# Late q turned by whole rows, and a reordered start, in a linear attention followed by a SwiGLU layer

## The chip, the core and the metric

The kernel runs on one core of a Trainium2 chip. The metric is the device time of one execution in microseconds (us), as the median of several runs; lower is better. Before the change it is 319.28 us, the median of three runs (319.25 to 319.5).

## The reference

Inputs are float32: q, k, v of 8 batches x 8 heads x 576 tokens x 64, a gain for the attention's norm, and the weights of the second layer. First a linear attention without softmax, with a root-mean-square norm over each head's 64 outputs:

```python
kv = np.einsum('bhsd,bhse->bhde', k, v)
out = np.einsum('bhsd,bhde->bhse', q, kv)
rms = np.sqrt(np.mean(out * out, axis=-1, keepdims=True) + 1e-06)
return (out / rms * g_norm).astype(np.float32)
```

Its result, laid out as 4608 tokens x 512, goes through a second norm and a gated feed-forward layer of width 1536:

```python
rms = np.sqrt(np.mean(x * x, axis=-1, keepdims=True) + 1e-06)
xn = x / rms * rms_g
g = xn @ w_gate
silu = g * (1.0 / (1.0 + np.exp(-g)))
val = xn @ w_val
return (silu * val @ w_out).astype(np.float32)
```

## The kernel before, in words

All products are in bf16 with float32 sums. The tokens go through the feed-forward part in nine groups of 512: the first 512 tokens of each of the 8 batches, and a last group of the 8 remainders of 64. Per group there are twelve pairs of a gate product and a value product (four products of 128 rows each, over the 512 channels), a Silu on ScalarE (ACT, L746), a multiplication on VectorE (DVE, L755), and then the output products (L773). While a group's feed-forward products run on TensorE (PE), the attention of the next batch is worked off in between; a planner (`Placer`) deals its operations out to slots. The change does not touch the planner.

For batch 0 there is nothing to hide behind. Its attention is written out by hand, line by line (L866 to L960), and this is the order in which each engine gets its instructions. Every engine works its own list in order; an instruction that waits holds up all that stand behind it on that engine. Batch 0 is done in two halves of 256 tokens: `part` 0 ("early", chunks 0 and 1) and `part` 1 ("late", chunks 2 and 3). The names below are those of the listing.

- `idle_on` (L900) and `spin` (L256) are products whose results nobody reads. `idle_on` takes data that has just landed, so such a product waits for it.
- `kv_pairs` makes k-transposed times v for a pair of heads; `qT_quads` (L325) turns q by products with the identity, in blocks of 64 rows x 64 columns, and `qT_out` (L360) copies the turned q out of PSUM.
- `oT_mm` (L452) makes the attention's output turned, only for the statistics: `sqT_` (L465) squares it on ACT, and `stat_pairs` (L472) sums the squares per head with a small product (L484).
- `o_pairs` (L422) makes the output itself in tiles `ox` and `oy`. `lead_chain` (L518) turns the sums into one factor per token and head: reciprocal, product, sum, product on DVE, a Sqrt on ACT (L533), a reciprocal on DVE. `xna_pairs` (L432) multiplies the output by that factor on DVE; `xT_mm` (L601) turns it on PE and `xT_out` (L614) copies it out, times the gain. Only then can the first gate products start (`gates`, L760).
- The late half goes through the same steps, but its factor is worked out by `chain` (L538), twelve small DVE steps without a Sqrt. `behind` (L985) puts these steps between the early half's feed-forward slots by a table, `steps`: after slot n, steps a to b.

Three PSUM pools bound what may run ahead: `att` (3 tiles), `mm1` (3) and `o2` (2). ACT holds one table of functions at a time: Sqrt's and Silu's differ, and `preload_act_table` (L948) loads Silu's. The weights come in eight transfers, gate and value in turn (`wg`, `wv`, three blocks of 128 columns each), issued by GpSimd (POOL) and converted on the way; all transfers of the start share the DMA engines. PE uses the first block's gate, then its value, then the second's, and so on; the first nine pairs run on the early half alone.

Of the kernel before, what the change touches and what calls it, by code (L numbers as in the profile page):

```python
# [11 lines left out]
BF16 = mybir.dt.bfloat16  # L12
# [75 lines left out]
def kernel(  # L88
# [12 lines left out]
    nc = tc.nc  # L101
    B, H, S, D = q.shape
# [3 lines left out]
    NC = 4  # L106
    MAIN = 128 * NC
# [25 lines left out]
    o2_p = pool("o2", 2, space=bass.MemoryType.PSUM)  # L133
    att_p = pool("att", 3, space=bass.MemoryType.PSUM)


    idle = consts.tile([128, MAIN], BF16, name="idle")
    nc.vector.memset(idle, 0.0)
    ident = consts.tile([128, 128], BF16, name="ident")
# [20 lines left out]
    krT = consts.tile([128, 2, H, D], BF16, name="remk")  # L160
    vr = consts.tile([128, H, 2, D], BF16, name="remv")
# [16 lines left out]
    mains, xs = {}, {}  # L178
# [77 lines left out]
    def spin(ps, n):  # L256
        for _ in range(n):
            nc.tensor.matmul(ps, lhsT=idle[:, :128], rhs=idle[:, : ps.shape[-1]], start=True, stop=True, skip_group_check=True)
# [4 lines left out]
    class Att:  # L263
# [61 lines left out]
        def qT_quads(self, part, halves, pools):  # L325
            tiles = [
                pool.tile([128, 2, MAIN // 2], BF16, name="o2" if pool is o2_p else "att") for pool in pools
            ]
            for c in range(NC):
                for h in range(H // 2):  # L330
                    for ps, hh in zip(tiles, halves):
                        rows, at = slice(hh * D, (hh + 1) * D), slice(h % 2 * D, (h % 2 + 1) * D)
                        nc.tensor.matmul(
                            ps[at, h // 2, c * D : (c + 1) * D],
                            lhsT=mains[0, 0][rows, part, h, c * D : (c + 1) * D], rhs=ident[rows, rows],
                            is_transpose=True, start=True, stop=True, skip_group_check=True,
                        )
            return tiles

        def turned(self):  # L340
            self.qT_ps = [att_p.tile([128, NS, MAIN // 2], BF16, name="att") for _ in range(2)]
            for c in range(NC):
                for h in range(H):
                    for r, ps in enumerate(self.qT_ps):
                        rows, at = slice(r * D, (r + 1) * D), slice(h % 2 * D, (h % 2 + 1) * D)
                        nc.tensor.matmul(
                            ps[at, h // 2, c * D : (c + 1) * D],
                            lhsT=qc[rows, h, c * D : (c + 1) * D], rhs=ident[rows, rows],
                            is_transpose=True, start=True, stop=True, skip_group_check=True,
                        )  # L350
# [517 lines left out]
    V, G, A = nc.vector, nc.gpsimd, nc.scalar  # L868
    H0, H1 = (0, 4), (4, 8)
    P0, P1 = (0, 1), (2, 3)  # L870
# [26 lines left out]
    idle_ps = mm1_p.tile([128, MAIN], FP32, name="mm1")  # L897
    spin(idle_ps, 17)

    def idle_on(rhs, n):  # L900
        for _ in range(n):
            nc.tensor.matmul(
                idle_ps[:, : 4 * D], lhsT=idle[: rhs.shape[0], :128], rhs=rhs,
                start=True, stop=True, skip_group_check=True,
            )

    idle_on(vr[:, 0:2].rearrange("p h c d -> p (h c d)"), 3)
    a = Att(0)
    cast_main(0, 1, V, H0)
    cast_main(0, 1, A, H1)  # L910
    V.tensor_copy(out=krT[: REM // 2], in_=krst.rearrange("p h (c d) -> p c h d", c=2))
    idle_on(mains[0, 1][:, 0, 4:8, :].rearrange("p h d -> p (h d)"), 4)
    idle_on(krT[:, 0, 0:4].rearrange("p h d -> p (h d)"), 2)
    kva = a.kv_pairs(P0)
    for i, j in enumerate(P0):
        a.kv_pairs_out(kva, i, j)
    idle_on(mains[0, 0][:D, 0, 0], 3)
    qa, qb = a.qT_quads(0, (0, 1), (att_p, att_p))
    a.qT_out(qa, P0, 0, A)
    a.qT_out(qb, P1, 0, V)  # L920
# [16 lines left out]
    )  # L937
    a.sqT_(a.oT_mm((3,), 0, 2, o2_p, 2), (3,), 0, 2)
    a.stat_pairs(P0, 0, 2, mm1_p, "mm1", guard=True)
    (la,) = a.qT_quads(1, (0,), (att_p,))  # L940
    a.stat_pairs(P1, 0, 2, mm1_p, "mm1")
    a.qT_out(la, P0, 2, A)
    ox = a.o_pairs(P0, 0, 2, att_p, "att")
    oy = a.o_pairs(P1, 0, 2, att_p, "att")
    a.lead_chain(0, 2, table=False)
    (lb,) = a.qT_quads(1, (1,), (att_p,))
    a.qT_out(lb, P1, 2, A)
    A.preload_act_table(ACT.Silu)  # L948
    xt = [a.xT_ps(1, (0, 1), pool_) for pool_ in (o2_p, None, None)]
    lo = [a.oT_mm(P0, 2, 4, o2_p), a.oT_mm(P1, 2, 4)]  # L950
    spin(mm1_p.tile([128, MAIN], FP32, name="mm1"), 2)
    xt.append(a.xT_ps(1, (0, 1), mm1_p))
    for o, js in ((ox, P0), (oy, P1)):
# [1 line left out]
            a.xna_pairs(o[:, :, 2 * i : 2 * i + 2], (j,), 0, 2)  # L955
    for j in ALL:
        a.xT_mm((j,), (0, 1), ps=xt[j])
        a.xT_out(j, (0, 1), A if j == 2 else V)
    for ps, js in zip(lo, (P0, P1)):
        a.sqT_(ps, js, 2, 4)  # L960

    for t in (0, 2, 1):
        load_cast(1, t, (0, H))
# [14 lines left out]
    for n, w in enumerate(FB):  # L978
        js = range(FB0[n], FB0[n] + w)
        early += [slots_a(0, j, 0, half)[0] for j in js if n] + [slots_a(0, j, 0, half)[1] for j in js]  # L980
    held = {}

    steps = {1: (0, 3), 2: (3, 6), 3: (6, 12)}

    def behind(n):  # L985
        if n == 1:
            a.st = None
            a.stat_pairs(P0, 2, 4, att_p, "att")
            a.stat_pairs(P1, 2, 4, att_p, "att")
        if n in steps:  # L990
            for f in a.chain(2, NC)[slice(*steps[n])]:
                f()
        if n in (3, 4):
            held[n - 3] = a.o_pairs((P0, P1)[n - 3], 2, 4, att_p, "att")
        if n == 6:
            for i, js in enumerate((P0, P1)):
                a.xna_pairs(held[i], js, 2, 4)
        if n in (10, 11):
            js = (P0, P1)[n - 10]
            a.xT_mm(js, (2, 3))  # L1000
            for j in js:
                a.xT_out(j, (2, 3), A)

    def lead(n0, n1):
        for n in range(n0, n1):
            if n == 12:
                gate = nc.sync.dma_start(out=gbc, in_=g_norm.partition_broadcast(128))
                tc.add_manual_dep(gate.ins, w_loads[-1][0].ins.name, SYNC, reason="the weights come first")
            emit([early[n]])
            behind(n)  # L1010
# [74 lines left out]
```

## Time and profile before

| | us |
|---|---|
| median of three runs | 319.28 (319.25 to 319.5) |
| the profiled execution | 319.22 |
| its span, first to last instruction | 317.5 |
| PE busy | 310.1 (98%) |
| DVE, ACT, POOL busy | 167.9, 139.1, 87.5 |

In stretches of the start, busy time of each engine in us (PEld is the loading of weights into PE's array; the DMA column is what the DMA engines moved):

| us of the span | PE | DVE | ACT | POOL | GB/s |
|---|---|---|---|---|---|
| 5 to 10 | 4.05 of 5 | 1.50 | 1.04 | 4.79 | 195 |
| 10 to 15 | 4.53 of 5 | 2.44 | 2.63 | 4.19 | 202 |
| 15 to 20 | 4.27 of 5 | 3.29 | 4.04 | 2.26 | 201 |
| 20 to 25 | 5.00 of 5 | 4.47 | 2.50 | 2.85 | 205 |
| 25 to 30 | 4.81 of 5 | 2.52 | 2.41 | 3.85 | 197 |

How to read the profile: a row of a timeline gives the start and the length in us, the engine, the line of the listing, the operation, the tiles as out<-in, sizes, a count, and in brackets the idle time before it with what ended it. Products on PE overlap, and their ends are modelled, so starts are the safer reading: the distance from start to start is what one costs in a row. The chain of waits goes back from the last instruction, at each step to what released it.

### The profile page before, as it was taken

How to read it: one execution, taken by the hardware profiler on the slowest of the kernel's cores; microseconds unless marked ns; L12 is line 12 of the kernel's file. 1: busy time of each engine (PE TensorE's matmuls, PEld its weight loads, DVE VectorE, ACT ScalarE, POOL GpSimd, SP SyncE). 2: the span in 40 equal slices, each digit the busy share in tenths (PEclk: the TensorE clock that was granted, in tenths of full speed). 3: DMA queues.
4: the chain of work that ended last, by engine and by line, in shares of the span. 5: the costliest groups of instructions: out<-in, count | busy, mean ns of one | idle time of the engine just before them, and what ended most of it. 6: DMA issues, size and time to landing. Idle time of an engine off the chain costs nothing.

```text
span 317.5 us, 5789 instructions
## 1 busy us (share of the span) xinstructions
PE 310.1 (98%) x2252; PEld 157.4 (50%) x2252; DVE 167.9 (53%) x379; ACT 139.1 (44%) x263; POOL 87.5 (28%) x108
## 2 busy tenths in 40 slices
PE   7899999999999999999999999999999999999995
PEld 3688855544454444444544454444444444444443
DVE  5475546579759643854196618561769034103310
ACT  2455364596477324631483237322842233233321
POOL 8846430067018301820085008400510000000000
PEclk9999999999999999999999999999999999999999
DMA  8999999999971994595439955954001600040002
GB/s 201 197 202 199 198 236 197 175 223 142 194 224 13 162 179 154 113 196 131 127 98 142 155 148 139 161 135 133 1 2 22 192 2 2 21 106 8 0 33 99
DMA packets 78358, 40.18 MB, mean 127 GB/s; under 512 B 43000, under 2 KB 73852, under 8 KB 78332
## 3 DMA queue, kind: packets, MB, share of 16 engines
q0 software_dynamic: 32304, 14.75, 36.6%
q1 hardware_dynamic: 45328, 24.48, 32.3%
q10 hardware_dynamic: 700, 0.59, 0.6%
q8 instruction: 17, 0.28, 0.4%
q14 instruction: 9, 0.07, 0.1%
HBM read 37.78 MB, written 9.44 MB: 149 GB/s over the span
## 4 chain that ended last, share of the span: by engine, by line
PE 93%; DMA 2%; ACT 1%; DVE 1%; POOL 1%; issue 1%; DVEq 0%; POOLq 0%
PE mm L737 58%; PE o L773 27%; DMA main_q<-in_q_dram 2%; PE mm L773 2%; PE att L294 2%; PE o L409 1%; PE att L409 1%; DVE xna L436 0%; PE mm L804 0%; PE o L804 0%; PE o L737 0%; PE att L608 0%; ACT x L618 0%; PE mm L766 0%; PE att L384 0%
## 5 line engine op out<-in xcount | busy, mean ns | idle before, releaser
L755 DVE TENSOR_TENSOR h<-silu,mm 128x512 bf16<-128x512 bf16 (+1 forms) x117 | 74.4, 636 | 87.5 <-PE mm L737 78.6
L746 ACT ACTIVATE silu<-mm 128x512 bf16<-128x512 f32 (+1 forms) x119 | 66.3, 558 | 85.6 <-PE mm L737 77.1
L737 PE MATMUL mm<-x,wv 128*128 128x512 bf16 (+1 forms) x420 | 98.2, 358 | 0.2 <-ACT silu L746 0.2
L737 PE MATMUL mm<-x,wg 128*128 128x512 bf16 (+1 forms) x420 | 98.4, 358 | 0.0
L773 PE MATMUL o<-wo,h 128*128 128x512 bf16 x396 | 90.1, 379 | 0.3 <-issue 0.3
L737 PEld LDWEIGHTS <-wv 128*128 128x128 bf16 x480 | 46.4, 98 | 45.7 <-issue 0.4
L737 PEld LDWEIGHTS <-wg 128*128 128x128 bf16 x468 | 45.5, 98 | 46.0
L501 POOL TENSOR_TENSOR sq<-sq,g 128x512 bf16<-128x512 bf16 x28 | 32.0, 1153 | 127.6 <-ACT sq L392 82.0
L773 PEld LDWEIGHTS <-h 128*128 128x128 bf16 x420 | 40.4, 98 | 47.5 <-issue 0.6
L793 ACT COPY osb<-o 128x512 f32<-128x512 f32 x33 | 19.2, 586 | 69.1 <-PE o L773 69.1
L509 DVE TENSOR_REDUCE st<-sq 128x8 f32<-128x512 bf16 x56 | 35.9, 677 | 0.0
L323 DVE CAST kvs<-att 64x256 bf16<-64x256 f32 x14 | 5.9, 422 | 30.8 <-PE att L294 30.6
L578 DVE TENSOR_TENSOR xna<-outa,al 128x512 bf16<-128x512 bf16 x24 | 15.1, 682 | 0.0
L737 PE MATMUL mm<-xr,wg 128*128 128x512 bf16 x48 | 12.3, 379 | 0.0
L737 PE MATMUL mm<-xr,wv 128*128 128x512 bf16 x48 | 12.3, 379 | 0.0
L229 POOL CAST main_q<-stg 128x1024 bf16<-128x1024 f32 x10 | 10.3, 1073 | 0.0
L200 POOL DMA_DIRECT2D vc<-in_v_dram x10 | 8.6, 862 | 2.7 <-DMA wv<-in_moe_w_val_dram 1.6
L893 ACT ACTIVATE wv<-wv,gain 128x384 bf16<-128x384 bf16 x16 | 9.0, 608 | 0.4 <-PE mm L737 0.4
L773 PE MATMUL mm<-wo,h 128*128 128x512 bf16 x24 | 7.6, 379 | 0.0
L446 ACT ACTIVATE sq<-att 128x512 bf16<-128x512 f32 x12 | 7.6, 633 | 0.0
L446 ACT ACTIVATE sq<-o 128x512 bf16<-128x512 f32 x12 | 7.3, 611 | 0.0
L200 POOL DMA_DIRECT2D kc<-in_k_dram x7 | 6.5, 932 | 2.9 <-DMA kc<-in_k_dram 1.7
(146 smaller groups left out, 188.4 us busy)
## 6 DMA issues: line engine op xcount, KB each, us to landing
out_dram<-osb SPq DMA_DIRECT2D x27, 256.0 KB, 2.5
stg<-in_q_dram SPq DMA_DIRECT2D x6, 1024.0 KB, 6.7
vc<-in_v_dram POOLq DMA_DIRECT2D x7, 512.0 KB, 8.1
kc<-in_k_dram POOLq DMA_DIRECT2D x7, 512.0 KB, 6.4
out_dram<-osb SPq DMA_DIRECT2D x17, 128.0 KB, 2.4
wg<-in_moe_w_gate_dram POOLq DMA_DIRECT2D x4, 384.0 KB, 10.4
wv<-in_moe_w_val_dram POOLq DMA_DIRECT2D x4, 384.0 KB, 11.6
wo<-in_moe_w_out_dram POOLq DMA_DIRECT2D x4, 384.0 KB, 14.4
```

Of the source, the lines that this page charges most:

```text
L200: return nc.gpsimd.dma_start(out=to[:, heads[0] : heads[1], : NC * D], in_=view)
L229: return copy(out=mains[b, t][:, cs[0] : cs[1], h0:h1, :], in_=staged[b, t].rearrange("p h (c d) -> p c h d", c=NC)[:, cs[0] : cs[1], h0:h ...
L446: nc.scalar.activation(out=self.sq[c][:, 0], in_=self.o_of(c), func=ACT.Square)
L501: eng.tensor_tensor(out=self.sq[c][:, 1], in0=self.sq[c][:, 0], in1=g2, op=OP.mult)
L509: nc.vector.reduce_sum(out=self.part(self.st[:, which], c), in_=of, axis=AX.X)
L578: return eng.tensor_tensor(out=self.part(self.xna, c), in0=of, in1=self.part(self.al, c).to_broadcast([128, 2, H // 2, D]), op=OP.mult,)
L737: nc.tensor.matmul(ps[:, : c1 - c0], lhsT=w[n][:, s, jj * 128 : (jj + 1) * 128], rhs=x_of(g, s, c0, c1), start=s == 0, stop=s == NS - 1)
L746: nc.scalar.activation(out=sis[g, j][:, c0:c1], in_=ps, func=ACT.Silu)
L755: nc.vector.tensor_tensor(out=hs[g, j][:, c0:c1], in0=sis[g, j][:, c0:c1], in1=v_ps, op=OP.mult)
L773: nc.tensor.matmul(ps, lhsT=hs[g, j][:, t * 128 : (t + 1) * 128], rhs=wo[j // OB][:, j % OB, :], start=j == 0, stop=j == NF - 1)
L793: (eng.copy if eng is nc.scalar else eng.tensor_copy)(out=o, in_=ps)
L893: A.mul(out=w[:, s], in_=w[:, s], mul=gain[:, s : s + 1])
```

## The change

- The first half's idle products: twelve of 256 columns become six of 512.
- Late q is turned by a new function, `qT_halves`: 16 products over all 128 rows in place of 32 in blocks of 64 x 64, into one tile `late` of pool `att`. It stands between `ox` and `oy`; before, one half stood between the two halves of the statistics and the other behind `lead_chain`.
- Both halves of late q are copied out by ACT behind the Sqrt of `lead_chain`; before, the first copy stood ahead of it.
- Late squares (`sqT_` of `lo`) stand ahead of the load of the Silu table; before, behind ACT's copy of the third x. The third of the four x tiles is allocated after `lo`.
- All four first x are copied out by DVE; before, the third by ACT.
- The statistics and the first chain steps of the late half come after slot 0 in place of slot 1, and the steps are dealt out as 4, 2, 2, 4 in place of 3, 3, 6.

```diff
+        def qT_halves(self, part):
+            ps = att_p.tile([128, 2, 2, MAIN // 2], BF16, name="att")
+            for c in range(NC):
+                for h in range(H // 2):
+                    at = slice(h % 2 * D, (h % 2 + 1) * D)
+                    nc.tensor.matmul(
+                        ps[at, :, h // 2, c * D : (c + 1) * D],
+                        lhsT=mains[0, 0][:, part, h, c * D : (c + 1) * D], rhs=ident,
+                        is_transpose=True, start=True, stop=True, skip_group_check=True,
+                    )
+            return ps
...
-                idle_ps[:, : 4 * D], lhsT=idle[: rhs.shape[0], :128], rhs=rhs,
-                start=True, stop=True, skip_group_check=True,
-            )
-
-    idle_on(vr[:, 0:2].rearrange("p h c d -> p (h c d)"), 3)
+                idle_ps, lhsT=idle[: rhs.shape[0], :128], rhs=rhs, start=True, stop=True, skip_group_check=True
+            )
+
+    idle_on(vr[:, 0:4].rearrange("p h c d -> p (h c d)"), 2)
...
-    idle_on(mains[0, 1][:, 0, 4:8, :].rearrange("p h d -> p (h d)"), 4)
-    idle_on(krT[:, 0, 0:4].rearrange("p h d -> p (h d)"), 2)
+    idle_on(mains[0, 1][:, 0].rearrange("p h d -> p (h d)"), 2)
+    idle_on(krT[:, 0].rearrange("p h d -> p (h d)"), 1)
...
-    idle_on(mains[0, 0][:D, 0, 0], 3)
+    idle_on(mains[0, 0][:D, 0, 0:2].rearrange("p h x -> p (h x)"), 1)
...
     a.stat_pairs(P0, 0, 2, mm1_p, "mm1", guard=True)
-    (la,) = a.qT_quads(1, (0,), (att_p,))
     a.stat_pairs(P1, 0, 2, mm1_p, "mm1")
-    a.qT_out(la, P0, 2, A)
     ox = a.o_pairs(P0, 0, 2, att_p, "att")
+    late = a.qT_halves(1)
     oy = a.o_pairs(P1, 0, 2, att_p, "att")
     a.lead_chain(0, 2, table=False)
-    (lb,) = a.qT_quads(1, (1,), (att_p,))
-    a.qT_out(lb, P1, 2, A)
+    a.qT_out(late[:, 0], P0, 2, A)
+    a.qT_out(late[:, 1], P1, 2, A)
+    xt = [a.xT_ps(1, (0, 1), pool_) for pool_ in (o2_p, None)]
+    lo = [a.oT_mm(P0, 2, 4, o2_p), a.oT_mm(P1, 2, 4)]
+    xt.append(a.xT_ps(1, (0, 1)))
+    for ps, js in zip(lo, (P0, P1)):
+        a.sqT_(ps, js, 2, 4)
     A.preload_act_table(ACT.Silu)
-    xt = [a.xT_ps(1, (0, 1), pool_) for pool_ in (o2_p, None, None)]
-    lo = [a.oT_mm(P0, 2, 4, o2_p), a.oT_mm(P1, 2, 4)]
     spin(mm1_p.tile([128, MAIN], FP32, name="mm1"), 2)
...
-        a.xT_out(j, (0, 1), A if j == 2 else V)
-    for ps, js in zip(lo, (P0, P1)):
-        a.sqT_(ps, js, 2, 4)
+        a.xT_out(j, (0, 1), V)
...
-    steps = {1: (0, 3), 2: (3, 6), 3: (6, 12)}
+    steps = {0: (0, 4), 1: (4, 6), 2: (6, 8), 3: (8, 12)}
 
     def behind(n):
-        if n == 1:
+        if n == 0:
             a.st = None
```

## The prediction

> **What bounds the kernel now.** I read the page first (busy shares, chain by line), then the chain of waits from 12.2 to 26.2 us, the timelines of PE, ACT and DVE over the same stretch, and last the issues of the weights with their time to landing.
>
> From the page:
>
> ```profile
> PE 310.1 (98%) x2252; PEld 157.4 (50%) x2252; DVE 167.9 (53%) x379; ACT 139.1 (44%) x263; POOL 87.5 (28%) x108
> ...
> PE 93%; DMA 2%; ACT 1%; DVE 1%; POOL 1%; issue 1%; DVEq 0%; POOLq 0%
> ```
>
> The span is TensorE's products. A change that leaves the products of the feed-forward part alone gains only where PE stands still. From 26.1 us on, the chain is PE products almost without a break, so everything is decided in the first 26 us. The chain of waits there (start, length, what):
>
> ```profile
> 13.11 0.18 PE mm L484 x4
> 13.29 0.37 PE att L333 x16
> 13.66 0.20 PE mm L484 x4
> 13.86 0.02 issue
> 13.88 0.27 DVE r L527
> ...
> 15.40 1.43 DVE xna L436 x4
> ...
> 25.26 0.50 ACT x L618
> 25.76 0.28 ACT silu L746
> 26.05 0.04 issue
> 26.09 0.27 PE mm L737
> ```
>
> The turn of half of late q (L333) lies on the path between the two halves of the statistics (L484); then DVE's chain and the four xna products follow. The end of this stretch is another engine: ACT's four late turns of x (L618) hold back a Silu, and PE waits for that Silu at 26.09. In between stands a transfer. The issues on POOL's timeline (start, length), from the view of DMA issues in a window inside each one its time to landing (last column), and PE's row of the product that uses the second:
>
> ```profile
> 11.08 0.75 POOL L248 DMA_DIRECT2D wg<-in_moe_w_gate_dram  x1
> 11.81 0.76 POOL L249 DMA_DIRECT2D wv<-in_moe_w_val_dram  x1
> ...
> wg<-in_moe_w_gate_dram POOLq DMA_DIRECT2D x1, 384.0 KB, 11.6
> ...
> wv<-in_moe_w_val_dram POOLq DMA_DIRECT2D x1, 384.0 KB, 12.9
> ...
> 24.86 1.03 PE L737 MATMUL mm<-x,wv 128*128 128x256 bf16 x8
> ```
>
> The third gate block lands at 11.08 + 11.6 = 22.68, the third value block at 11.81 + 12.9 = 24.7. PE's first product with the gate block starts at 23.01, with its weight load at 22.91: 0.2 us to spare. Its first product with the value block starts at 24.86 (weight load 24.72), where the products before it (four from 24.33, 0.109 each) would have let it start at 24.77. PE already stands at that landing. Whatever is gained ahead of it can pass only through the wait behind it.
>
> **The change, part by part.**
>
> **Idle products.** Out go 3 + 4 + 2 + 3 = 12 of 256 columns at 0.109 us (1.31), in come 6 of 512 at 0.216 (1.30). The last ones before each real product end ahead of a DMA: v at 8.57 (0.30 of wait in PE's row) and q's second half at 10.06 (the chain's 3.44 + 6.62). Cost 0; without that cover 0.1 at most.
>
> **Statistics in one run.** The 16 turns go from between the halves: 0.37 in the chain. The second half then needs the square of j = 3, which ends at 13.20; the first half ends at 13.29 in the chain. So the second half ends about 0.38 earlier and DVE's reciprocal starts at 13.50 in place of 13.88; if the semaphore of that square comes later than I take it, the gain is 0.34. DVE's chain and Sqrt keep their lengths: Sqrt 14.41 to 14.63 (was 14.79), xna from 15.01 and its last end at 16.43 (was 16.82).
>
> **Late q in whole rows.** 32 products of 64 rows x 64 columns become 16 that take all 128 rows and give 128 columns each. No such row is in the trace. The nearest: L333 itself, 16 in 0.25 without the changes of shape (starts 13.22 to 13.47); L294 (128 rows, 64 columns, two column halves in turn), 40 in 0.76, two per 0.038; L426 (128 columns, no halves) 0.055 each. The bounds for 16 are 0.25 and 16 x 0.055 = 0.88; I take pairs side by side like L294's with L426's width, 8 x 0.057 = 0.46, and two changes of shape of 0.07 to 0.1 (L333's first and last neighbours). It is in PE's order after `ox` and before `oy`: 13.62 to 14.07, read by ACT from about 14.3. `oy` ends by 14.5 (15.0 at the other bound), xna needs it at 15.7: covered.
>
> **Sqrt ahead of both copies.** On ACT before: copy 13.70, Sqrt 14.79, copy 14.92 to 15.48. After: Sqrt to 14.63, copies from 14.53 and 15.01 (start to start 0.12 and 0.48, as L533 to L364 and L470 to L470 show), the second to 15.58. So the second late copy ends 0.10 later although everything else is earlier. What is queued behind it on PE: `lo[1]` (2 x 0.109), the two spins (2 x 0.216), and only then the turns of x. The first turn starts at 16.28 (was 16.18), DVE's first x is then at 16.59 instead of 16.73, released by PE and no longer by its own xna, and ends at 16.93; the gates start at 16.98 instead of 17.13. Of 0.38, **0.15 is left**. If the wide turns run one after another, copies shift 0.14 and nothing is left; if the copies do not overlap (0.57 + 0.57 from 14.63) the second ends at 15.77, 0.04 worse than no gain.
>
> **x of j = 2 on DVE.** ACT loses 0.47, DVE gains 0.26 (its start to start). The fourth x ends at 17.71; the gates need it in their last quarter, nine products after 16.98, at 17.96. Cost 0, with 0.25 to spare.
>
> **Late squares ahead of the Silu table.** ACT: squares from 15.57 and 16.06 to 16.65, the table load (1.28) to 17.94; the first Silu is wanted when the first gate ends, 16.98 + 9 x 0.109 + 0.27 = 18.23. Cost 0, with 0.3 to spare; before, the Silu at 18.50 came straight behind these squares.
> [...]
>
> ```profile
> 15.50 1.28 ACT L948 ACT_TABLE_LOAD   x1
> 17.18 0.47 ACT L618 ACTIVATE x<-att,gain 128x256 bf16<-128x256 bf16 x1 [0.40 <-PE att L608]
> ```
>
> The load starts 0.02 behind the copy before it, and the next ACT operation comes 0.40 behind its end, waiting for PE. So a pause after a load is between 0 and 0.40; I take 0. [...]
>
> **Statistics and chain of the late half one slot earlier.** The 8 products (0.20) stand ahead of the first value block instead of behind it: same PE work. On DVE the four steps (0.2, 0.3, 0.2, 0.2) now run from 18.67, ahead of the first h, which goes from 19.14 to about 19.57; the second h ends at 20.61 (was 20.47). The fifth gate (20.83, waits for DVE) would start at 20.68: it just fits. The late xna starts at 22.07 instead of 22.53, off the path.
>
> **Through the two landings.** The gates' lead of 0.15 survives the gate block (weight load 22.77 against 22.68). At the value block PE still starts at 24.86. But ACT's run that ends at 26.04 begins when that gate's product ends (23.65), so it ends 0.15 earlier; eight products from 24.86 end their issue at 25.74, so PE's next starts at 25.94 instead of 26.09. After that PE runs on without a wait to 41.50, the next transfers being 1 us and more ahead of it. **Sum: 0.15 less.** The profiled execution took 319.22 (span 317.5), the three runs 319.28 in the median, 0.06 more: 319.1 either way.
>
> **The rivals.**
> **A, slower: ACT's queue holds PE.** Either the second late copy ends after 15.73 (then the gates start later than 17.13) or the Silu table is ready after 18.28. [...] Both pass on to the end, since PE has only 0.09 in hand at the value block: 319.3 to 319.5. For it: ACT now has two copies and two squares in a row with PE products queued behind each. Against: the rows show copies overlapping and no pause over 0.40.
> **B, the pause at 41.50 goes or moves.** The chain shows 0.34 of "issue" there (start to start 0.51 more than a product), with no waiting semaphore named; PE has 22 products fewer ahead of it, so it can fall elsewhere. Gone with the 0.15: 319.22 - 0.65 = 318.6. For: nothing in the rows ties it to data. Against: nothing says that it depends on the count.
> **C, the landings come earlier too** or ACT's run shrinks: the whole 0.36 (24.86 + 0.88 = 25.74 to 26.09) plus 0.09 at the value block: 318.8. Against: POOL issues the weights by 13.3, before anything changes.
> **D, much slower: PE's pace.** The windows' table has 7 idle products in 1 to 4 us and 11 in 4 to 6, at a granted clock of 1.00 in both: a half pace that the clock column does not show. If thinner work ahead of 17 us brought it back, it decides from some gap longer than the 0.46 of idle time before 6.79, which left the pace whole; the longest that the change makes is about 0.7 (14.4 to 15.15, `oy` to `lo[0]`). Price: about 2.8 us at half pace (1.2 to 4.0 was needed to leave it), 1.4 lost: 320.6. [...]
>
> **How the numbers follow.** Forecast 0.48 (its own range 319.0 to 319.25), A 0.20, B 0.14, C 0.08, D and further pauses 0.10. About 0.2% (0.64 us) is what a measurement of this kernel can tell from no change. Only B (most of it, 0.11) and a bit of C (0.01) go past it as faster, D as slower: 0.12, 0.78, 0.10. The range takes in the forecast, A with its bounds, C and B's 318.6, up to 319.7 for a pause on top of A; it leaves out D and the far end of B.
>
> **What would show it.** Reciprocal at 13.5; Sqrt at 14.4 with two copies behind; first turn of x not before 16.2; gates at 17.0; the product with the third value block still at 24.8 to 24.9; the Silu wait at 26.09 shortened by about as much as the gates moved. Wrong if that block lands elsewhere, if the wide turns take over 0.9 us, or if a new PE wait above 0.2 stands between 17 and 24 us.

## The result and the profile after

The changed kernel takes 318.62 us in the median of 20 runs (318.3 to 319.15), the kernel before 319.39 in 20 runs beside them: a ratio of 0.9976, 95% interval 0.9969 to 0.9983, or 0.77 us less (0.54 to 0.99). The time lies in the range, at its low end, and on the faster side of the bound of 0.2%, across which the interval reaches. That is the place of rival B, which had a chance of 0.14; the likeliest case had its own range of 319.0 to 319.25 and was missed. The range held because its lower end was set by B. Both profiled executions of experiment 6 ran with PE at a reduced pace (spans 329.1 and 654.5 us), and such executions are left out of the ratios.

The profiled execution took 318.71 us (before 319.22), its span 316.9 (317.5). From its page:

```profile
PE 308.4 (97%) x2208; PEld 156.6 (49%) x2230; DVE 168.1 (53%) x380; ACT 138.8 (44%) x262; POOL 87.6 (28%) x108
...
PE 94%; DMA 2%; ACT 1%; issue 1%; DVE 0%; POOL 0%; POOLq 0%
```

The chain of waits in the start of the changed kernel (start, length, what), with what answers to the rows shown of before:

```profile
13.17 0.40 PE mm L496 x8
13.57 0.02 issue
13.59 0.27 DVE r L539
...
14.50 0.22 ACT nt L545
14.72 0.97 ACT qTs L376 x2
15.69 0.04 issue
15.73 0.38 PE att L471 x2
...
25.73 0.28 ACT silu L758
26.02 0.04 issue
26.06 0.38 PE mm L749 x2
```

The statistics (now L496) are one run of eight, and the reciprocal starts 0.29 earlier. Behind the Sqrt (L545) the chain no longer goes on through DVE's xna: it goes through ACT's two copies of late q (L376) to PE's second pair of late outputs (L471), as the prediction had it. And at 26.06 stands the same wait for a Silu, 0.03 us earlier than before. So the start gave nearly nothing. The half microsecond is elsewhere. The same view around the first output products, first of before, then of the changed kernel:

```profile
41.29 0.21 PE o L773
41.50 0.34 issue
41.85 0.38 PE o L773
42.23 0.22 PE mm L773
```

```profile
41.25 0.21 PE o L785
41.47 0.05 issue
41.52 0.38 PE mm L785
41.90 0.43 PE att L471 x2
```

The pause in which no semaphore is waited for is gone. (The changed trace lacks the record of the second output product; the third starts at 41.52, on time.) To split the difference of the two profiled executions, I take four marks that every kernel has: ACT's first copy of q (10.60 before, 10.66 after), PE's first product behind the Silu wait (26.09, 26.06), the first output product (41.12, 41.09) and the end of the span.

| stretch, us | before | after | difference |
|---|---|---|---|
| up to the first copy of q | 10.60 | 10.66 | +0.06 |
| to the product behind the Silu wait | 15.49 | 15.40 | -0.09 |
| to the first output product | 15.03 | 15.03 | 0 |
| to the end | 276.3 | 275.8 | -0.5 |

The first row is mostly the landing of the first transfers; in the experiments below it lies between 10.3 and 11.5, and it is left out when kernels are compared. Between the first copy and the reciprocal a late landing of v added 0.24 us in experiment 7, and the reciprocal came 0.10 later in experiment 2, so the distance from DVE's reciprocal to the first gate product is the safer reading of the front: 3.24 before, 3.50 in the changed kernel. The two profiled executions differ by 0.51, the medians by 0.77; the interval begins at 0.54, and what lies between is not attributed.

### The profile page after: what moved, and what is told of

It is laid out like the page before. It is cut to its first block, busy times and chain, and to the rows that moved or that the text cites. A ratio compares the mean times of both kernels' runs of the same rounds, so it can differ in the third digit from the quotient of the medians.

```text
span 316.9 us, 5724 instructions
## 1 busy us (share of the span) xinstructions
PE 308.4 (97%) x2208; PEld 156.6 (49%) x2230; DVE 168.1 (53%) x380; ACT 138.8 (44%) x262; POOL 87.6 (28%) x108
## 4 chain that ended last, share of the span: by engine, by line
PE 94%; DMA 2%; ACT 1%; issue 1%; DVE 0%; POOL 0%; POOLq 0%
PE mm L749 58%; PE o L785 27%; DMA vc<-in_v_dram 2%; PE mm L785 2%; PE att L294 2%; PE o L421 1%; PE att L421 1%; ACT qTs L376 0%; PE o L749 0%; PE mm L816 0%; PE o L816 0%; PE att L620 0%; PE att L471 0%; ACT x L630 0%; PE mm L778 0%
## 5 line engine op out<-in xcount | busy, mean ns | idle before, releaser
L785 PE MATMUL o<-wo,h 128*128 128x512 bf16 x382 | 87.5, 379 | 1.1 <-issue 0.6
L749 PE MATMUL mm<-xr,wv 128*128 128x512 bf16 x47 | 12.3, 379 | 0.1
L749 PE MATMUL mm<-xr,wg 128*128 128x512 bf16 x47 | 12.3, 379 | 0.1
```

The lines of the kernel that those rows point to most:

```text
L749: nc.tensor.matmul(ps[:, : c1 - c0], lhsT=w[n][:, s, jj * 128 : (jj + 1) * 128], rhs=x_of(g, s, c0, c1), start=s == 0, stop=s == NS - 1)
L785: nc.tensor.matmul(ps, lhsT=hs[g, j][:, t * 128 : (t + 1) * 128], rhs=wo[j // OB][:, j % OB, :], start=j == 0, stop=j == NF - 1)
```

## Experiments

The question was what the pause hangs on, and what each part of the change does to the front. Ratios are to the kernel before, run beside each; they are not simply the quotients of the medians. Each kernel has one profiled execution from which the stretches are read.

**1. Wide idle products alone.** The kernel before with `idle_on` of the changed one:

```diff
-    idle_on(vr[:, 0:2].rearrange("p h c d -> p (h c d)"), 3)
+    idle_on(vr[:, 0:4].rearrange("p h c d -> p (h c d)"), 2)
...
```

> The kernel before with one part of the change alone: six idle products of 512 columns in place of twelve of 256; all else as before, 6 products fewer on PE. Theory F (the gain is what PE is ahead at the wait for the Silu near 26.1 us): no change, within 0.1 us of before, the Silu wait ends at 26.1 and the pause near 41.4 stays. Theory P (the gain is the pause of 0.5 us between the first two output products near 41.4, and it depends on how many instructions PE has been given before): the pause may move or go with 12 instructions fewer; if it goes, 0.5 us faster. Theory L (that pause comes and goes with the time at which transfers land): it comes and goes without regard to the kernel, and the time is that of before within 0.1 us.

Ratio 0.9988 (0.9976 to 1.0001). The front is that of before to 0.01 (6.53 us from the first copy of q to the gates, 15.49 to the product behind the Silu wait). But the pause has moved. The chain of this kernel:

```profile
42.57 0.22 PE mm L773
42.78 0.22 PE o L773
43.00 0.14 issue
43.14 0.39 PE o L773
```

It is shorter (0.14 of issue) and stands six products further on in the program. Six products fewer had been given to PE.

**2. The changed kernel with the narrow idle products**, the reverse edit.

> The changed kernel with the twelve narrow idle products of before (6 products more on PE than in the changed kernel). F and L: as the changed kernel, 0.7 to 0.8 us faster than before. P: if the pause near 41.4 depends on the count of instructions, it may be back with 12 more, and then only 0.2 to 0.3 us faster than before.

Ratio 0.9979 (0.9966 to 0.9992), no pause, 275.8 from the first output product to the end. Sixteen products fewer than before are enough. The front of this execution was no faster than before (6.53 and 15.53): its reciprocal came 0.10 later after the first copy of q than in the changed kernel, and from there to the gates it took the same 3.50.

**3. The changed kernel with PE's count restored.**

```diff
     spin(idle_ps, 17)
+    spin(idle_ps[:, :16], 22)
```

> The changed kernel with 22 idle products of 16 columns more, behind the first 17 idle products, where PE waits for data anyway: PE's count of products is that of before, 44 instructions more than in the changed kernel. F and L: as the changed kernel, 0.7 to 0.8 us faster than before. P: the pause of 0.5 us near 41.4 is back at the same product, and the kernel is within 0.3 us of before.

Ratio 1.0007 (0.9994 to 1.0019): the whole gain is gone, and the pause is back at the same product, longer than before:

```profile
41.44 0.22 PE o L785
41.66 0.70 issue
42.36 0.39 PE o L785
```

The front is that of the changed kernel to 0.06 (6.49 and 15.45). Counted through each trace, the paused product has the same number in all three kernels that have a pause, though it is another product of the program in the second (number, start, line, tiles; in the changed kernel the same number falls on a product of the statistics):

```
before:         478  41.85  L773 o<-wo,h
wide idle:      478  43.14  L773 o<-wo,h
count restored: 478  42.36  L785 o<-wo,h
changed:        478  44.86  L506 att<-sel,sqT
```

So in these three kernels the pause goes with a place in PE's list of instructions, not with any data. And it is the whole difference behind the first output product: 276.33 less 0.51 before, 276.12 less 0.30 in experiment 1 and 276.69 less 0.87 here (from start to start, beyond a product's own 0.22) are all 275.82, the stretch of the kernels without a pause.

**4. The first parts of the change alone:** wide idle products, late q by whole rows, statistics in one run, Sqrt first; squares, x and chain steps as before.

```diff
-    for ps, js in zip(lo, (P0, P1)):
-        a.sqT_(ps, js, 2, 4)
     A.preload_act_table(ACT.Silu)
...
-        a.xT_out(j, (0, 1), V)
+        a.xT_out(j, (0, 1), A if j == 2 else V)
+    for ps, js in zip(lo, (P0, P1)):
+        a.sqT_(ps, js, 2, 4)
...
-    steps = {0: (0, 4), 1: (4, 6), 2: (6, 8), 3: (8, 12)}
+    steps = {1: (0, 3), 2: (3, 6), 3: (6, 12)}
```

> The changed kernel without its last two parts: late squares stand behind the Silu table again, the third x is copied by ACT again, and the late statistics and chain steps come after slot 1 in 3, 3 and 6 as before. What is left of the change: wide idle products, late q by whole rows, statistics in one run, Sqrt ahead of both copies. F: the gates start as early as in the changed kernel (17.0 to 17.1), but the squares are ACT's again just ahead of the first Silu, so part of the gain at 26.1 goes: 0.3 to 0.8 us faster than before. P and L: PE has the changed kernel's count, no pause near 41.4, at least 0.5 us faster than before.

Ratio 0.9980 (0.9969 to 0.9991), no pause, 6.43 and 15.39 from the first copy of q: the front of the changed kernel to 0.01. The late squares ahead of the table, the third x on DVE and the earlier chain steps are worth nothing here. This kernel also answers what stands behind a table load. ACT's timeline:

```profile
15.88 1.28 ACT L958 ACT_TABLE_LOAD   x1
17.18 0.47 ACT L630 ACTIVATE x<-att,gain 128x256 bf16<-128x256 bf16 x1
```

The load ends at 17.16 and the next operation starts at 17.18, 0.02 later.

**5. The kernel before with 106 products more** and nothing of the change:

```diff
-    spin(idle_ps, 17)
+    spin(idle_ps, 8)
+    spin(idle_ps[:, :64], 115)
```

> The kernel before, with 106 idle products more and nothing of the change: 8 of 512 and 115 of 64 columns in place of the first 17 of 512, about as long in all. [...] Theory W (the 22 products fewer of the change make PE earlier or its list shorter as such): the list is longer, so the pause stays or grows and the time is that of before or more.

No pause; PE's timeline of this kernel runs through the first output products without a gap, two of them in 0.43 us:

```profile
41.57 0.60 PE L737 MATMUL mm<-x,wv 128*128 128x256 bf16 x4
42.01 0.59 PE L773 MATMUL o<-wo,h 128*128 128x512 bf16 x2
42.44 0.38 PE L773 MATMUL mm<-wo,h 128*128 128x512 bf16 x1
```

275.8 to the end, with the old front (6.53 and 15.49). The time is that of before: ratio 0.9996 (0.9983 to 1.0008), since the many small products kept PE busy until 8.81 (6.3 before) and pushed the first copy of q to 11.49, 0.89 later, which gave back what the pause had cost. A longer list without the pause contradicts theory W. The 478th product is another one here and starts at 39.80.

**6. The kernel before with 30 products more**, 16 of 512 and 31 of 16 columns in place of 17 of 512, run twice.

> The kernel before with 30 idle products more (16 of 512 and 31 of 16 columns in place of the first 17 of 512). [...] W: the pause stays where it is, within 0.2 us of before.

> The same kernel as in the run with 30 idle products more, whose profiled execution was at a lower granted clock and cannot be read. [...] W: the pause stands at the same output product as before.

Ratios 1.0000 (0.9988 to 1.0012) and 1.0003 (0.9987 to 1.0020). A pause longer by 1 us than that of before would have shown (0.3%); there is none. Theory W had this time, but where a pause stands, if there is one, can't be seen: no stretch of this kernel can be read. With 30 products more the products ahead of the 478th are others too (see below). Why the time is that of before, and not half a microsecond less, stays open.

**7. Late q by whole rows alone**, at its old place between the halves of the statistics, the first copy ahead of the Sqrt (not shown: the second copy reads the same tile, and the second and third x tiles are allocated after `lo`):

```diff
-    (la,) = a.qT_quads(1, (0,), (att_p,))
+    late = a.qT_halves(1)
     a.stat_pairs(P1, 0, 2, mm1_p, "mm1")
-    a.qT_out(la, P0, 2, A)
+    a.qT_out(late[:, 0], P0, 2, A)
...
```

> The kernel before with late q turned by whole rows alone, at the old place between the halves of the statistics, and the first copy ahead of the Sqrt as before; twelve narrow idle products, squares, table, x and chain as before. 16 products fewer on PE. [...] F (the front makes the gain): 0.1 to 0.2 us slower than before.

Ratio 0.9981 (0.9969 to 0.9992). No pause (275.8), and a front that is slower by 0.47: 7.00 to the gates, 15.96 to the product behind the Silu wait. But 0.24 of that is not the edit's. It stands ahead of the turn, at products that take v, for whose transfer PE waited there in this execution and not in that of before:

```profile
11.26 0.38 PE L310 MATMUL mm<-vc,main_k 128*128 128x128 bf16 x4 [0.44 <-DMA vc<-in_v_dram]
```

The edit's own part is the turn between the halves of the statistics, 0.57 in place of 0.37 in the chain of waits, 0.2 more; from the reciprocal to the gates it is 3.24 as before. A kernel whose start is worse than before is faster than before.

**8. Both copies ahead of the Sqrt**, in the changed kernel:

```diff
-    a.lead_chain(0, 2, table=False)
     a.qT_out(late[:, 0], P0, 2, A)
     a.qT_out(late[:, 1], P1, 2, A)
+    a.lead_chain(0, 2, table=False)
```

> The changed kernel with both copies of late q ahead of the Sqrt on ACT: the step that puts the Sqrt first undone, and nothing else. Late q is turned by 14.3, so the copies hold ACT from about 14.35 to 15.4 and the Sqrt starts 0.8 later than now; the late outputs come 0.3 earlier, but the first x then waits for DVE's xna again: gates at 6.9 to 7.1 from the first copy of q in place of 6.43, the Silu wait behind them later by the same, 0.4 to 0.6 us slower than the changed kernel and 0.1 to 0.4 faster than before, with no pause at the output products (same count). If the order on ACT is worth nothing, as the changed kernel.

Ratio 0.9994 (0.9981 to 1.0006), 7.05 and 16.02: 0.62 behind the changed kernel in both, and 4.12 from the reciprocal to the gates in place of 3.50, with no pause. The Sqrt waits for the copies:

```profile
14.79 1.07 ACT L376 COPY qTs<-att 128x512 bf16<-128x512 bf16 x2 [1.14 <-PE att L345]
15.75 0.23 ACT L545 ACTIVATE nt<-z 128x16 f32<-128x16 f32 x1
```

So this order is what keeps the wide turn from making the front slower.

**9. Without the two idle products ahead of the turns of x**, in the changed kernel (the tile is still taken).

```diff
-    spin(mm1_p.tile([128, MAIN], FP32, name="mm1"), 2)
+    mm1_p.tile([128, MAIN], FP32, name="mm1")
```

> The changed kernel without the two idle products between the late outputs and the first turns of x (0.43 of PE ahead of those turns; 2 products fewer). If PE's order behind the second late copy holds the gates, as the prediction has it, the first turn of x starts 0.3 to 0.4 earlier and the gates 0.1 to 0.2 earlier, until DVE's own xna holds the first x (16.53): 6.2 to 6.35 from the first copy of q to the gates in place of 6.43. Up to the end 0 to 0.15 us faster than the changed kernel, as the landings of the third weights let pass. If DVE's chain holds the gates, no change.

6.35 to the gates, 15.32 to the product behind the Silu wait; ratio 0.9975 (0.9961 to 0.9988). From the reciprocal to the gates it is 3.42 in place of 3.50, and the chain goes through DVE's xna again (15.14). So 0.08 of the gates' lead did hang on PE's order behind the second copy, at the small end of what was expected. At the end of the kernel so little does not show in the ratio.

**10. Two late copies of x on DVE**, in the changed kernel.

```diff
-                a.xT_out(j, (2, 3), A)
+                a.xT_out(j, (2, 3), V if j % 2 else A)
```

> The changed kernel with two of the four late copies of x on DVE in place of ACT. If ACT's run of copies and Silus is what PE waits for at 26.06 (0.45 from start to start more than a product), that run gets about 0.7 shorter, DVE sits idle for 1.1 there, PE's next product starts 0.3 to 0.45 earlier against the start of the first copy of q (15.40 now, 15.0 to 15.1 then), and the kernel is 0.3 to 0.45 us faster than the changed one, 1.0 to 1.2 faster than before. If the third value block's landing (24.6) is what counts, nothing.

Ratio 0.9969 (0.9955 to 0.9984), 15.27. The Silu wait is gone, and in its place the chain of this kernel names the transfer:

```profile
12.10 12.77 DMA wv<-in_moe_w_val_dram
24.87 0.05 issue
24.91 1.59 PE mm L749 x13
```

It gained 0.13 in place of 0.3 to 0.45: the rest stops at the third value block, which landed at 24.87 (24.57 in the changed kernel's execution).

**11. Both of the last two.**

> The changed kernel with two late copies of x on DVE and without the two idle products, both together. Each alone took 0.1 off the front and met the third value block's landing; together no more than that landing lets pass: 15.1 to 15.3 from the first copy of q to the product behind the Silu wait, and 0.1 to 0.3 us faster than the changed kernel, no pause at the output products.

Ratio 0.9953 (0.9936 to 0.9971), 318.37 us against 319.51 beside it, 15.18 from the first copy of q. It has the lowest ratio here, from four executions; its interval touches that of the changed kernel, and of the 0.7 us by which the two ratios differ the marks account for 0.22. Its chain has the same transfer in the same place:

```profile
11.92 12.73 DMA wv<-in_moe_w_val_dram
24.65 0.05 issue
24.69 1.81 PE mm L749 x15
```

Behind it PE runs without a wait to the first output product (15.03). At this place the start of these two kernels is bound by the weights' transfers.

## Why the prediction was right or wrong, point by point

- **Idle products at no cost**: right for the front (experiment 1: 6.53 and 15.49 as before). That they move every later instruction of PE by twelve rows was not in the sum.
- **Statistics in one run, 0.38**: the reciprocal came 0.29 earlier, 0.35 against the first copy of q, which was 0.06 late. Right, near the lower bound of 0.34 that the prediction named.
- **Late q by whole rows, 8 pairs of 0.057 and two changes of shape**: 0.57 from the first wide turn (13.73) to the product behind it (14.30), against 0.46 and 0.07 to 0.1 twice. Right: 0.57 for all 16, where 16 x 0.055, one after another, would have been 0.88.
- **Sqrt ahead of both copies: 0.15 of the lead is left**: the mechanism was right, the chain goes through the second copy (15.67, predicted 15.58), PE's late outputs and idle products to the first turn of x (16.38, predicted 16.28). The size was 0.10 (6.53 to 6.43): the reciprocal came 0.35 earlier, and the way from it to the gates grew by 0.26 (3.24 to 3.50), in each of the five executions with this order (after, 2, 3, 4, 10). Experiment 8 gives the step's own worth, 0.62.
- **Third x, late squares, chain steps at no cost**: right, to 0.01 (experiment 4). The second h started at 20.19 and the late xna at 22.05 (predicted end of that h 20.61, start of that xna 22.07).
- **No pause behind the table load**: the load ended at 16.76 + 1.28 = 18.04, and the first Silu, at 18.38, waited 0.34 for PE, not for the table. The upper end of rival A's 319.3 to 319.5 takes in a pause behind the load that no run shows; experiment 4 shows the next operation 0.02 us behind the load's end. Rival A did not happen.
- **The lead through the landings**: the third value block landed at 12.27 + 12.3 = 24.57, its first product started at 24.73 without waiting, and 0.09 reached the product behind the Silu wait (predicted 0.15). That the landing is the wall behind a faster start was right: experiments 10 and 11 run into it.
- **Rival D, PE's pace**: did not happen. PE's longest waits from 6 to 17 us are 0.55 in the changed kernel (ahead of 7.16 and of 15.24; 0.46 before), and its first gate products behind them cost 0.109 each, as before. What ends the half pace from 1 to 4 us (7 products of 512 columns in 3 us, where a product costs 0.216 later), or would bring it back, no run of this case shows.
- **"So everything is decided in the first 26 us", and the pause as a constant of the sum**: this is the step that failed. The sum carried the 0.51 us pause at 41.50 unchanged, on the ground that "nothing says that it depends on the count", and gave its going a chance of 0.14 as rival B. The answer to that doubt is experiments 1, 3 and 5. The lead of the front, to which the sum gave all of the gain, is 0.09 of it. With that 0.09 and the pause in the sum the forecast for the profiled execution would have been 319.22 - 0.09 - 0.51 = 318.62; it took 318.71.

**What the pause is.** Shown, by one profiled execution of each kernel: where there is one, it stands ahead of PE's 478th product, which is not the same product of the program in all three (before, experiments 1 and 3), there is none near the first output products when the 478th is another product (2, 4, 5, 7 to 11), and its length is not fixed (0.14, 0.34 and 0.70 of issue). Beside it in the traces: queue 8, named "instruction", moves 17 packets of 16,384 bytes in the kernel before, where PE's list has some 4,500 rows (2252 products and 2252 loadings of weights). What the packets hold is not shown. The third packet of that queue starts 2.6 to 2.85 us after PE loads the weights of its 350th product, 128 products ahead of the 478th, in all twelve kernels whose profile can be read. In us:

| kernel | PE at its 350th | third packet | PE's 478th starts | after the packet's end |
|---|---|---|---|---|
| before | 37.00 | 39.64 to 40.66 | 41.85, behind the pause | 1.19 |
| 1, wide idle | 37.86 | 40.65 to 41.65 | 43.14, behind the pause | 1.49 |
| 3, count restored | 37.16 | 39.82 to 40.79 | 42.36, behind the pause | 1.57 |
| changed | 38.85 | 41.66 to 42.72 | 44.86 | 2.14 |
| 2, narrow idle | 38.57 | 41.16 to 42.16 | 44.33 | 2.17 |
| 7, whole rows alone | 39.44 | 42.22 to 43.18 | 45.20 | 2.02 |
| 5, 106 more | 25.98 | 28.58 to 29.47 | 39.80 | 10.3 |

The three kernels with the pause start their 478th product 1.19 to 1.57 us behind the packet's end, the four others of the table 2.02 us and more. Whether PE waits for that packet is not shown. What differs between the kernels is how long the 128 products from the 350th on take. In the kernel before, 104 of them are the short products of batch 1 (64 turns in 0.64 us, 40 products in 0.76), and the way from the 350th to the weights of the 478th takes 4.1 us; in the changed kernel the same numbers lie 22 products further on in the program, take in 16 products of 0.22 in place of one, and the way takes 6.0. In experiment 6 the same numbers lie 30 products earlier, and the 128 products at that place take 6.0 us in the trace of the kernel before (33.73 to 39.77): if a way of 6.0 us goes without a pause, as in the changed kernel, there was none in experiment 6 either; that is an estimate from these two traces. Not settled: what starts such a transfer; the fourth packet starts 4.9 us after the loading for the 478th product in the kernel before and 4.1 in the changed one.

## What to carry to other kernels

A pause of a bound engine with no semaphore behind it belongs in the sum with a question mark of its own: count the products up to it (here 477, in three kernels), and ask what the change does to that count and, by my reading of the table above, to how fast the products just ahead of it go by (4.1 us with the pause, 6.0 without). To attribute a small gain, split the span at marks that all versions have, and pad the changed kernel back to the old count; here the edits that were worked out in detail gave 0.09 us, and the fewer products on PE (16 are enough) gave 0.5. And a lead that is won ahead of a transfer is worth what the transfer lets pass: in experiments 10 and 11 PE's product stood 0.04 us behind the landing of its weights (24.87 and 24.65).

## What was not expected of the hardware

PE, waiting for no semaphore that the profile shows, stood still for 0.51, 0.30 and 0.87 us (start to start, beyond a product's own 0.22) ahead of its 478th product, in the kernel before and in experiments 1 and 3. With six products fewer the pause stood six products further on in the program (experiment 1), with sixteen fewer there was none (experiment 2). An ACT operation followed a table load by 0.02 us (experiment 4).
